# Second expert stage in three token groups instead of two, and the last expert block's result made by halves of its columns

## The chip, the cores and the metric

The kernel runs on one core of one Trainium2 chip. The core has a matrix engine (TensorE, PE in the profile, with its weight loads as PEld), VectorE (DVE), ScalarE (ACT), GpSimd (POOL) and SyncE (SP), which issues most of the transfers. Each engine works through its own list of instructions in order and waits for others by semaphores. The metric is the device time in microseconds (us) of one execution. A difference of about 1% is what a measurement of this kernel can tell from none.

## The reference

Three stages follow one another on 1536 tokens (2 x 768) of width 512:

```python
x = _attn_ref(q, k, v, n_sink, window)      # 8 heads of 64, a window of 128 and 4 sink keys
x = _moe_ref(x, w_skip, w_gate, w1, w2)     # first expert stage: 8 experts, 512 -> 1024 -> 512
h = x @ w_in                                # second expert stage: (1536, 512) @ (512, 2048)
g = np.where(h > 0.0, h, np.exp(np.minimum(h, 0.0)) - 1.0)
out = (g @ w_out).astype(np.float32)        # (1536, 2048) @ (2048, 512)
```

In the first expert stage a token with a positive skip score goes through the one expert that it scores highest on, and the gated result is added to it; the others stay as they are. `w_in` and `w_out` arrive as 64-bit floats, since the draw multiplies them by a 64-bit scalar.

## The kernel before

**First expert stage.** There are nine blocks of 128 tokens: one for each expert, and a ninth (number 8) for the tokens of one expert that did not fit. A block gathers its rows from the table `xtab` in DRAM, transposes them, makes the hidden layer in two halves (`layer1`, L902), applies the ReLU, makes the result in two halves of the hidden width (`layer2`, L918, the operations `b2`; all 512 columns in one PSUM bank), multiplies by the gate, and scatters the rows back to `xtab`. These matmuls are in float32, which TensorE runs as two records each.

**Second expert stage.** Each operand is split into a high and a low part in the type fp32r, and three products stand for one float32 product (`PASSES`). The 2048 hidden columns are 16 chunks of 128. The tokens are worked in groups (`GT`, 768 before, so two groups of six tiles of 128). For a group and a chunk, `l1` (L1083) makes the chunk's hidden values for the group's tokens, in two halves of 384 tokens (12 matmuls each, into one of two PSUM banks); five `elu` operations on ACT and DVE (L1095 or L1097, L1099, L1102, L1104, L290) turn them into the two parts of `gt`; `l2` (L1119, three matmuls of 512 columns for each token tile) adds the chunk's part to the six sums, which fill six banks for the whole group. `l2` of a chunk comes one chunk behind `l1`.

**Between the stages.** The first group's tokens do not wait for block 8's scatter. They are read from `xtab` before it (`lx0`, L986, two transfers of 384 rows), transposed into PSUM (`x0t`, L1016), and block 8's contribution is added there by matmuls with a one-hot matrix (`x0a`, L1021), which needs block 8's gated result as `delta` in two parts (L1000 on ACT, then L1002 on DVE). The sums are then split into `xT` (L1030 on ACT, L1032 on DVE). A later group's rows are loaded (L1040), transposed (L460 from L1042) and split (L1049, L1051) when the group before it is through `l1`.

**Weights of the second stage.** `w_in` and `w_out` are converted from 64-bit words on the chip, chunk by chunk: two loads (L736, L738), and for each of the two 128 x 512 halves one ACT operation (L960), five DVE operations (L962, L963, L964, L966, L290) and a cast (L968, ACT or DVE). The first ten chunks are converted beside the expert blocks, the rest beside the first group of the second stage.

**What sets the order.** Every operation is given to a planner (`Plan`) with its costs per engine, what it follows, a priority and the buffers that it takes. The planner goes through time and writes out one fixed order per engine; the chip keeps that order. `kinds` lists the buffers: `X`, `ACC` and `L1` are sets of PSUM banks, `g` and `r` rings in SBUF.

Of the kernel before, what the change touches and what calls it, by code (L numbers as in the profile page):

```python
# [8 lines left out]
F32 = mybir.dt.float32  # L9
F32R = mybir.dt.float32r  # L10
# [165 lines left out]
def fused_kernel(  # L176
# [28 lines left out]
    GT = 768  # L205
# [83 lines left out]
    def sub(o, a, b, e):  # L289
# [589 lines left out]
    def block(e):  # L879
# [16 lines left out]
        for n in range(2):  # L896
# [18 lines left out]
            def layer2(eng, n=n):  # L915
                for f in range(4 * n, 4 * n + 4):
                    w = w_tile(("w", e, KD + f // 2)).rearrange("p (c n) -> p c n", c=2)
                    nc.tensor.matmul(bk(("y", e)), sl(post["hT"], ("hT", e))[:, f, :], w[:, f % 2, :], start=(f == 0), stop=(f == KF - 1))  # L918
            add(("b2", e, n), {"e": 3.45}, layer2, [("relu", e, n)] + [("w", e, KD + 2 * n + i) for i in range(2)] + ([("b2", e, 0)] if n else []), p0 + 2 + n,
                need=[] if n else [("Y", ("y", e), 3 if last else 1)], use=[("hT", e)] + [("w", e, KD + 2 * n + i) for i in range(2)])  # L920
# [3 lines left out]
        add(("out", e), {"d": 0.69}, result, [("b2", e, 1)] + ([("dl", 0), ("dl", 1)] if last else []), p0 + 4, use=[("y", e), ("xg", e)])  # L924
# [50 lines left out]
    NS = NI // 2  # L975
    GH = GT // 2
    ohr = {}
    xTs = {}
    L8 = NB - 1

    def x0_tile():
        return post["exb"][:, 0:3072].rearrange("p (n j d) -> p n j d", n=2, j=NS)

    def load_x0(e, n):
        r0 = 1 + n * GH
        nc.sync.dma_start(out=x0_tile()[:, n], in_=xtab[r0:r0 + GH, 0:DM].rearrange("(j p) d -> p j d", p=P))  # L986

    def tokens_hot(e, n):
        if not n:
            post["oh"] = post["bp"].tile([P, 2 * GH], F32R, tag="c", name="oh")  # L990
        ohr[n] = post["oh"][:, n * GH:(n + 1) * GH]
        for j in range(NS):
            i = n * NS + j
            nc.vector.tensor_scalar(out=ohr[n][:, j * P:(j + 1) * P], in0=iota, scalar1=tok6[:, i:i + 1], scalar2=None, op0=ALU.is_equal)

    def delta(e, part):
        y, gt = bk(("y", L8)), gates(L8)
        if part == 0:
            post["dl"] = post["bp"].tile([P, 2, DM], F32R, tag="hs", name="delta")
            nc.scalar.activation(out=post["dl"][:, 0], in_=y, func=ACTF.Copy, scale=gt)  # L1000
        else:
            nc.vector.scalar_tensor_tensor(out=post["dl"][:, 1], in0=y, scalar=gt, in1=post["dl"][:, 0].bitcast(F32), op0=ALU.mult, op1=ALU.subtract)  # L1002
# [34 lines left out]
    for i in range(NI):
        def load_x(e, i=i):
            r0 = 1 + GT + i * P
            nc.sync.dma_start(out=post["row"][i][:, 0:DM], in_=xtab[r0:r0 + P, 0:DM])  # L1040
        add(("lx", i), {"s": 0.45}, load_x, [("scat", L8)] + [("cv", NCH - 1, w, 6) for w in range(2)] + ([("lx", i - 1)] if i else []), 310.0, size=262144)
        add(("xt", i), {"e": 0.44}, lambda e, i=i: four(post["row"][i], bk(("xt", i), 4), ident), [("lx", i)] + [("l1", 0, NCH - 1, i // NS)], 315.9 + 0.01 * i, need=[("L1", ("xt", i), 2)])  # L1042

        def x_ev(e, part, i=i):
            n, j = divmod(i, NS)
            m = bk(("xt", i), 4)
            o = xTs[n][:, :, :, j * P:(j + 1) * P]
# [464 lines left out]
```

## Time and profile before

| | us |
|---|---|
| median of three runs | 545.1 (543.37, 545.1, 547.71) |
| the profiled execution, its time | 546.95 |
| its span, first to last instruction | 545.2 |
| TensorE busy | 524.4 (96%) |
| VectorE busy | 317.8 (58%) |
| ScalarE busy | 190.1 (35%) |

Times in the rows are from the start of the span. The granted TensorE clock is 1.00 of full speed (2.4 GHz) throughout the stretches that are shown. In rows of a timeline, the second number is the length of the stretch from the first instruction's start to the last one's end; a bracket gives the idle time before it and what ended it. A matmul's own duration is longer than the step from one matmul to the next, because they are pipelined; steps are read as differences of starts.

### The profile page before, as it was taken

Reading aid. Unit: us, or ns where it says so; the run is one execution under the profiler, and the core shown is the slowest. Engines: PE = TensorE matmul, PEld = TensorE weight load, DVE = VectorE, ACT = ScalarE, POOL = GpSimd, SP = SyncE. Lnnn points to the kernel's source line nnn. Section 1 sums busy time; section 2 is a strip of 40 time slices with the busy share of each in tenths; the row PEclk is TensorE's granted clock in tenths of the full one; section 3 lists DMA queues with packets and bytes.
Section 4 is the critical chain, followed back from the end, with each engine's and each line's share of the span. In section 5 each row is a group of like instructions: output and inputs, shape, how many; then the busy total and the mean of one; then the engine's idle time right before and its main releaser. Section 6 shows DMA issues by size and latency. Waiting matters only on the chain.

```text
span 545.2 us, 8684 instructions
## 1 busy us (share of the span) xinstructions
PE 524.4 (96%) x3271; PEld 439.7 (81%) x3271; DVE 317.8 (58%) x887; ACT 190.1 (35%) x467; POOL 30.4 (6%) x46
## 2 busy tenths in 40 slices
PE   8999989988999999999899999999999999999994
PEld 4778767878777777777799899899989989999893
DVE  6777676875211468978999843433565344353442
ACT  3877566840000023433666521211232121121120
POOL 2000000011111011000001000000000000000000
PEclk9999998997999999999999999999999999999998
DMA  9999999319999868756545100000030000000003
GB/s 171 261 272 338 271 282 289 97 32 364 396 393 398 295 201 264 267 169 237 172 152 155 62 20 1 0 1 1 0 117 0 1 1 1 0 1 0 1 2 121
DMA packets 73141, 79.14 MB, mean 145 GB/s; under 512 B 43073, under 2 KB 51521, under 8 KB 73090
## 3 DMA queue, kind: packets, MB, share of 16 engines
q1 hardware_dynamic: 69810, 73.29, 43.3%
q0 software_dynamic: 1520, 4.99, 2.7%
q8 instruction: 28, 0.46, 0.4%
q10 hardware_dynamic: 1760, 0.22, 0.3%
q14 instruction: 23, 0.19, 0.1%
HBM read 69.82 MB, written 8.66 MB: 144 GB/s over the span
## 4 chain that ended last, share of the span: by engine, by line
PE 87%; DMA 9%; DVE 1%; ACT 1%; issue 1%; SPq 0%; ACTq 0%; DVEq 0%
PE bank L1083 24%; PE bank L1119 24%; PE bank L902 11%; PE bank L918 10%; DMA pl<-in_k_dram 4%; PE bank L572 4%; PE bank L531 4%; PE bank L460 3%; PE bank L603 2%; DMA raw<-in_moe_w_in_dram 2%; PE bank L559 1%; PE bank L577 1%; DMA pl<-in_q_dram 1%; PE bank L558 1%; DMA pl<-xtab,gid 1%; DMA xtab<-r,sidx 1%
## 5 line engine op out<-in xcount | busy, mean ns | idle before, releaser
L1083 PE MATMUL bank<-xT,m 128*128 128x384 f32 x768 | 139.3, 336 | 1.9 <-DVE xT L1051 1.0
L1083 PEld LDWEIGHTS bank<-xT,m 128*128 128x128 f32 x768 | 134.7, 188 | 4.8 <-ACT xT L1049 1.2
L1119 PE MATMUL bank<-m,gt 128*128 128x512 f32 x576 | 137.9, 392 | 0.0
L1119 PEld LDWEIGHTS bank<-m,gt 128*128 128x128 f32 x576 | 107.4, 188 | 21.0
L1099 ACT ACTIVATE re<-re 128x384 f32<-128x384 f32 x64 | 33.6, 525 | 143.7 <-DVE re L1097 142.7
L1097 DVE TENSOR_SCALAR re<-bank 128x384 f32<-128x384 f32 x28 | 15.6, 558 | 88.2 <-PE bank L1083 88.1
L902 PEld LDWEIGHTS bank<-blk,pl 128*128 128x128 f32 x480 | 57.1, 197 | 3.7 <-issue 2.6
L902 PE MATMUL bank<-blk,pl 128*128 128x128 f32 x480 | 58.0, 281 | 0.6 <-ACT blk L345 0.6
L918 PE MATMUL bank<-pl,blk 128*128 128x512 f32 x128 | 57.6, 592 | 0.0
L1102 DVE SCALAR_TENSOR_TENSOR re<-re,bank 128x384 f32<-128x384 f32 x64 | 35.4, 553 | 28.2 <-ACT re L1099 27.9
L545 ACT ACTIVATE pw<-sm,rm 128x272 f32<-128x272 f32 (+2 forms) x96 | 47.1, 495 | 7.0 <-DVE rm L537 7.0
L960 ACT ACTIVATE r<-raw 128x512 f32<-128x512 f32 x32 | 21.3, 678 | 62.4 <-DMA raw<-in_moe_w_in_dram 51.9
L918 PEld LDWEIGHTS bank<-pl,blk 128*128 128x128 f32 x128 | 23.1, 190 | 23.0 <-issue 23.0
L537 DVE CUSTOM_DVE_ANT_0 sm<-bank,mk 128x272 f32<-128x272 f32 (+2 forms) x96 | 35.2, 406 | 6.8 <-PE bank L531 4.8
L290 DVE TENSOR_TENSOR gt<-re,gt 128x384 fp32r<-128x384 f32 x61 | 34.0, 558 | 1.8
L1095 ACT ACTIVATE re<-bank 128x384 f32<-128x384 f32 x36 | 17.7, 491 | 32.4 <-PE bank L1083 32.4
L531 PE MATMUL bank<-kt,pl 64*128 64x272 f32 (+2 forms) x192 | 28.4, 418 | 0.0
L572 PE MATMUL bank<-PT,pl 128*64 128x128 f32 x352 | 25.2, 285 | 0.1
L345 ACT COPY PT<-bank 128x512 f32<-128x512 f32 (+1 forms) x40 | 20.6, 550 | 13.0 <-PE bank L559 10.7
L572 PEld LDWEIGHTS bank<-PT,pl 128*64 128x64 f32 x352 | 19.3, 139 | 5.9 <-issue 3.1
L966 DVE SCALAR_TENSOR_TENSOR r<-raw,r 128x512 int32<-128x512 int32 x32 | 22.6, 712 | 0.3
L290 DVE TENSOR_TENSOR m<-r,m 128x512 fp32r<-128x512 f32 x32 | 21.6, 689 | 1.6 <-ACT m L968 1.1
(186 smaller groups left out, 529.6 us busy)
## 6 DMA issues: line engine op xcount, KB each, us to landing
pl<-in_moe_w_dram SPq DMA_DIRECT2D x62, 512.0 KB
raw<-in_moe_w_in_dram SPq DMA_DIRECT2D x16, 512.0 KB
raw<-in_moe_w_out_dram SPq DMA_DIRECT2D x16, 512.0 KB
pl<-in_k_dram SPq DMA_DIRECT2D x12, 256.0 KB
pl<-in_q_dram SPq DMA_DIRECT2D x12, 256.0 KB
pl<-in_v_dram SPq DMA_DIRECT2D x12, 256.0 KB
xtab<-pl SPq DMA_DIRECT2D x12, 256.0 KB
out_dram<-raw SPq DMA_DIRECT2D x5, 512.0 KB
```

The costliest lines, as they stand in the source:

```text
L290: CE[e].tensor_tensor(out=o, in0=a, in1=b, op=ALU.subtract)
L531: nc.tensor.matmul(o, qT[r, p, :], rhs, start=True, stop=True)
L537: nc.vector.tensor_tensor_reduce(out=sl(sm_t, ("sm", t, h))[:, 0:n], in0=bk(("s", t, h))[:, 0:n], in1=m, scale=-scale, scalar=3.0e38, op0= ...
L545: nc.scalar.activation(out=sl(pw_t, ("pw", t))[:, h, 0:n], in_=sl(sm_t, ("sm", t, h))[:, 0:n], func=ACTF.Exp, bias=rm[:, t, h:h + 1], scal ...
L572: nc.tensor.matmul(o[i * D:(i + 1) * D, p, :], vt[:, h * D:(h + 1) * D], pT[:, (0 if y else c - 2) + i, :], start=(p == 0 and (y == 1 or n ...
L902: nc.tensor.matmul(o[:, i, :], w_tile(("w", e, kk))[:, f * P:(f + 1) * P], sl(post["xT"], ("xT", e))[:, kk, :], start=(i == 0 and kk == 0) ...
L918: nc.tensor.matmul(bk(("y", e)), sl(post["hT"], ("hT", e))[:, f, :], w[:, f % 2, :], start=(f == 0), stop=(f == KF - 1))
L966: add(nm(4), {"d": 0.69}, lambda e, ai=ai, r=r: nc.vector.scalar_tensor_tensor(out=ai(), in0=r()[:, :, 0], scalar=29, in1=ai(), op0=ALU.lo ...
L1083: nc.tensor.matmul(pt, w[:, a, kk, :], xTs[n][:, b, kk, :], start=(i == 0), stop=(i == 3 * KD - 1))
L1099: nc.scalar.activation(out=r, in_=r, func=ACTF.Exp, scale=-1.0)
L1102: nc.vector.scalar_tensor_tensor(out=r, in0=r, scalar=-1.0, in1=pt, op0=ALU.add, op1=ALU.max)
L1119: nc.tensor.matmul(bk(("acc", g, i)), gt[:, a, i % NS * P:(i % NS + 1) * P], w[:, b, :], start=(c == 0 and j == 0), stop=(c == NCH - 1 and ...
```

## The change

The group is 512 tokens, so there are three groups of four tiles. One `l1` operation then covers a whole chunk of a group: 12 matmuls of 512 columns. The sums of a group fill four banks (`ACC`, 0 to 3) and `l1` has four (`L1`, 4 to 7). `l2` gets the priority of two chunks behind `l1`; the ring `g` has three buffers of 512 tokens. `xT` is kept in six pieces, one for each 128 input columns (`XT`), so that a later group's pieces take turns with the earlier group's; `l1` is cut into two halves of the input columns for chunks 0 to 2 of the first group and chunk 0 of the others, so that its first half waits for two pieces only. A later group's transposes are placed within the last chunks of the group before, and its rows are loaded without waiting for the conversion of the weights.

In block 8 `layer2` is made in four pieces: both halves of the hidden width for result columns 0 to 255, then both for 256 to 511. `delta` and the one-hot matmuls follow by halves of the columns. The first group's rows come in one transfer of 512 rows.

```diff
-    GT = 768
+    GT = 512
...
-        S=B_(0, 1, 2, 3), T=B_(4, 5, 6, 7), O=B_(4, 5, 6, 7), HB=B_(0, 1, 2, 3), Y=B_(4, 5), T2=B_(6, 7), X=B_(*range(8)),
-        ACC=B_(0, 1, 2, 3, 4, 5), L1=B_(6, 7),
+        S=B_(0, 1, 2, 3), T=B_(4, 5, 6, 7), O=B_(4, 5, 6, 7), HB=B_(0, 1, 2, 3), Y=B_(4, 5), T2=B_(6, 7), X=B_(0, 1, 2, 3),
+        ACC=B_(0, 1, 2, 3), L1=B_(4, 5, 6, 7),
...
-        xg=ring(4, INF), xT=ring(2, INF), hT=ring(2, INF), a=ring(2, INF), r=ring(2), g=ring(5), row=ring(6, INF), o2=raws,
+        xg=ring(4, INF), xT=ring(2, INF), hT=ring(2, INF), a=ring(2, INF), r=ring(2), g=ring(3), XT=ring(6), row=ring(6, INF), o2=raws,
...
+            else:
+                add(("b2", e, 0) if n else ("b2x", e), {"e": 1.75}, lambda eng, n=n: layer2(eng, range(4 * n, 4 * n + 4), slice(0, DM // 2)), [("relu", e, n)] + ws + ([("b2x", e)] if n else []), p0 + 2 + n,
+                    need=[] if n else [("Y", ("y", e), 5)])
+                if n:
+                    for h in range(2):
+                        add(("b2", e, 1) if h else ("b2y", e), {"e": 1.75}, lambda eng, h=h: layer2(eng, range(4 * h, 4 * h + 4), slice(DM // 2, DM)), [("b2y", e) if h else ("b2", e, 0)], p0 + 4 + h,
+                            use=[("hT", e)] + [("w", e, KD + 2 * h + i) for i in range(2)])
...
-    for n in range(2):
-        add(("hot", n), {"d": 0.6}, lambda e, n=n: tokens_hot(e, n), ["tok6", "aend"], PB - 9)
-        add(("lx0", n), {"s": 0.45}, lambda e, n=n: load_x0(e, n), [("scat", L8 - 1), ("b2", 6, 1)], PB - 9, size=786432)
-    add(("dl", 0), {"a": 0.69}, lambda e: delta(e, 0), [("b2", L8, 1)], PB + 3.5, use=[("y", L8)])
-    add(("dl", 1), {"d": 0.74}, lambda e: delta(e, 1), [("dl", 0)], PB + 3.5, use=[("y", L8)])
+    add("hot", {"d": 0.9}, tokens_hot, ["tok6", "aend"], PB - 9)
+    add("lx0", {"s": 0.45}, load_x0, [("scat", L8 - 1), ("b2", 6, 1)], PB - 9, size=1048576)
+    for h in range(2):
+        add(("dl", 0, h), {"a": 0.37}, lambda e, h=h: delta(e, 0, h), [("b2", L8, h)], PB + 3.5, use=[("y", L8)])
+        add(("dl", 1, h), {"d": 0.41}, lambda e, h=h: delta(e, 1, h), [("dl", 0, h)], PB + 3.5, use=[("y", L8)])
...
+        def x0_add(e, a, kk=kk, key=key):
+            nc.tensor.matmul(bk(key), post["dl"][:, a, kk * P:(kk + 1) * P], post["oh"], start=False, stop=(a == 1))
+        add(("x0b", kk), {"e": 0.23}, lambda e, f=x0_add: f(e, 0), [("x0t", kk), "hot", ("dl", 0, kk // 2)], PB + 3.9 + 0.01 * kk)
+        add(("x0a", kk), {"e": 0.23}, lambda e, f=x0_add: f(e, 1), [("x0b", kk), ("dl", 1, kk // 2)], PB + 4 + 0.01 * kk)
+        split(0, kk, key, PB + 5 + 0.01 * kk, [("x0a", kk)] + ([("b2", L8, 1)] if kk > 1 else []))
...
+            add(("xt", g, kk), {"e": 0.44}, xt, [("lx", g, i) for i in range(NI)] + [("l1", g - 1, NCH - 1 - (kk < 2))], pr - 2.5 + kk * 0.6, need=[("L1", ("xt", g, kk), 2)])
+            split(g, kk, ("xt", g, kk), pr - 2.5 + kk * 0.6, [("xt", g, kk)])
...
+        if c < (1 if g else 3):
+            for h in range(2):
+                kks = (2 * h, 2 * h + 1)
+                add(name if h else ("l1k", g, c), {"e": 1.36}, lambda e, kks=kks: l1(e, kks),
...
-            add(("l2", g, c, i), {"e": 0.70}, l2, [("elu", g, c, i // NS, 4), ("cv", c, 1, 6)] + ([("l2", g, c - 1, i)] if c else []), p0 + 1.3 + 0.01 * i,
+            add(("l2", g, c, i), {"e": 0.68}, l2, [("elu", *key, 4), ("cv", c, 1, 6)] + ([("l2", g, c - 1, i)] if c else []), p0 + 2.3 + 0.01 * i,
```

The order that the planner writes is the same on every engine up to the end of block 8's hidden layer, but for two one-hot operations fewer on VectorE and one transfer in place of two. What it moves is shown at three places. In the changed kernel the lines are numbered otherwise: L1040 is the first group's transpose (L1016 before), L1044 the one-hot matmul (L1021), L1089 `l1` (L1083), L1127 `l2` (L1119), L1061 a later group's transpose (L460). `exb` holds the first group's rows, `blk` the hidden values of block 8, `m_` numbers a chunk's weights (the lowest number is chunk 0), `r_1488` to `r_1493` are row buffers.

TensorE at the end of block 8, before:

```order
L918 MATMUL bank_93<-pl_64,blk 128x512 x4
L1016 MATMUL bank_95<-ident,exb 128x128 x3
...
L918 MATMUL bank_93<-pl_65,blk 128x512 x4
L1016 MATMUL bank_94<-ident,exb 128x128 x3
...
L1021 MATMUL bank_95<-oh,delta 128x384 x2
...
L1083 MATMUL bank_95<-xT_2275,m_1874 128x384 x12
L1083 MATMUL bank_96<-xT_2275,m_1918 128x384 x12
L1083 MATMUL bank_95<-xT_2297,m_1874 128x384 x12
L1119 MATMUL bank_90<-m_1874,gt 128x512 x3
```

and in the changed kernel:

```order
L918 MATMUL bank_93<-pl_64,blk 128x256 x4
L918 MATMUL bank_93<-pl_65,blk 128x256 x4
L1040 MATMUL bank_90<-ident,exb 128x128 x4
...
L1044 MATMUL bank_91<-oh,delta 128x512
L918 MATMUL bank_93<-pl_64,blk 128x256 x4
L1044 MATMUL bank_90<-oh,delta 128x512
L1044 MATMUL bank_91<-oh,delta 128x512
L918 MATMUL bank_93<-pl_65,blk 128x256 x4
L1044 MATMUL bank_92<-oh,delta 128x512
L1044 MATMUL bank_89<-oh,delta 128x512
L1089 MATMUL bank_95<-xT_2269,m_1872 128x512 x6
L1044 MATMUL bank_92<-oh,delta 128x512
```

All 16 transposes now stand ahead of the last two quarters of block 8's result, the first columns' one-hot matmuls stand between these quarters, and nothing stands between the last quarter and the next columns' one-hot matmuls. From there `l1` of chunks 0 to 4 comes ahead of the first `l2`.

VectorE in the first group, while weights are still converted (L962 to L966 before are L972 to L976 now, L1102 is L1110), before and then in the changed kernel:

```order
L1102 SCALAR_TENSOR_TENSOR re<-re,bank_95 128x384
L966 SCALAR_TENSOR_TENSOR r_1493<-raw_83,r_1493 128x512
L962 TENSOR_SCALAR r_1492<-r_1492 128x512
L290 TENSOR_TENSOR gt<-re,gt 128x384
L290 TENSOR_TENSOR m_2337<-r_1493,m_2337 128x512
L963 TENSOR_SCALAR r_1492<-r_1492 128x512
L1102 SCALAR_TENSOR_TENSOR re<-re,bank_96 128x384
```

```order
L1110 SCALAR_TENSOR_TENSOR re<-re,bank_96 128x512
L290 TENSOR_TENSOR m_2384<-r_1492,m_2384 128x512
L974 SCALAR_TENSOR_TENSOR r_1493<-raw_85,r_1493 128x512
L290 TENSOR_TENSOR gt<-re,gt 128x512
L976 SCALAR_TENSOR_TENSOR r_1493<-raw_85,r_1493 128x512
L972 TENSOR_SCALAR r_1492<-r_1492 128x512
L1110 SCALAR_TENSOR_TENSOR re<-re,bank_94 128x512
L290 TENSOR_TENSOR m_2384<-r_1493,m_2384 128x512
L973 TENSOR_SCALAR r_1492<-r_1492 128x512
```

From one L1110 to the next there are now one `gt` and some five operations of a conversion (four in these rows, six in the next stretch), which is one half of a chunk's weights for each chunk of the group.

TensorE at the change of group, before and then in the changed kernel (`m_2665` and `m_2630` are the last chunk's weights):

```order
L1119 MATMUL bank_94<-m_2665,gt 128x512 x3
L460 MATMUL bank_96<-ident,r_1491 128x128 x4
L1119 MATMUL bank_92<-m_2665,gt 128x512 x3
L1119 MATMUL bank_89<-m_2665,gt 128x512 x3
L460 MATMUL bank_95<-ident,r_1492 128x128 x4
L1119 MATMUL bank_93<-m_2665,gt 128x512 x3
L460 MATMUL bank_96<-ident,r_1493 128x128 x4
L1083 MATMUL bank_95<-xT_2275,m_1874 128x384 x12
```

```order
L1061 MATMUL bank_95<-ident,r_1491 128x128
L1127 MATMUL bank_91<-m_2444,gt 128x512 x3
L1127 MATMUL bank_92<-m_2444,gt 128x512 x3
L1127 MATMUL bank_89<-m_2444,gt 128x512 x3
L1089 MATMUL bank_96<-xT_2269,m_2630 128x512 x9
...
L1061 MATMUL bank_93<-ident,r_1491 128x128
L1127 MATMUL bank_91<-m_2511,gt 128x512 x3
L1127 MATMUL bank_92<-m_2511,gt 128x512 x3
L1127 MATMUL bank_89<-m_2511,gt 128x512 x3
L1089 MATMUL bank_95<-xT_2301,m_1872 128x512 x6
```

Where the next group's `l1` came straight behind the last transpose, nine `l2` matmuls and more now stand between each pair of transposes and the `l1` that needs them.

## Rows read from the trace of the kernel before

**Rows 1.** The page: busy time of each engine, and the chain that ended last, by engine

```profile
PE 524.4 (96%) x3271; PEld 439.7 (81%) x3271; DVE 317.8 (58%) x887; ACT 190.1 (35%) x467; POOL 30.4 (6%) x46
PE 87%; DMA 9%; DVE 1%; ACT 1%; issue 1%; SPq 0%; ACTq 0%; DVEq 0%
```

**Rows 2.** Busy time by stretch: PE, PEld, DVE, ACT, POOL, clock, DMA share, GB/s

```profile
280.23:313.40 33.17, 33.17 (x170) 30.20 (x169) 29.73 (x57) 20.65 (x39) 3.61 (x3) 1.00 0.38 120
313.40:396.53 83.13, 83.13 (x423) 75.65 (x422) 35.69 (x71) 15.42 (x30) 0.00 (x0) 1.00 0.02 4
404.36:537.50 133.14, 133.10 (x672) 120.89 (x672) 59.15 (x117) 25.24 (x49) 0.00 (x0) 1.00 0.02 8
```

**Rows 3.** Chain that ended last, chunks 2 and 15 of the first group: start, us

```profile
280.23 4.18 PE bank L1083 x24
284.42 4.12 PE bank L1119 x18
...
388.20 4.18 PE bank L1083 x24
```

**Rows 4.** Who waited for whom, TensorE from 253 to 540: total, times, longest

```profile
PE bank L1083 <- DVE xT L1051: 1.0, 1, 1.0
PE bank L1083 <- DVE re L1102: 0.9, 1, 0.9
PE bank L1021 <- DVE delta L1002: 0.6, 1, 0.6
```

**Rows 5.** Timeline of block 8's end: start, us, engine, line, [idle before, releaser]

```profile
246.05 7.31 PE L902 MATMUL bank<-blk,pl 128*128 128x128 f32 x64
253.20 3.60 PE L918 MATMUL bank<-pl,blk 128*128 128x512 f32 x8
256.21 0.14 PEld L1016 LDWEIGHTS bank<-ident,exb 128*128 128x128 f32 x1 [0.24 <-DMA exb<-xtab]
256.63 1.47 PE L1016 MATMUL bank<-ident,exb 128*128 128x128 f32 x12
257.94 3.60 PE L918 MATMUL bank<-pl,blk 128*128 128x512 f32 x8
261.38 1.15 PE L1016 MATMUL bank<-ident,exb 128*128 128x128 f32 x9
261.64 0.67 ACT L1000 ACTIVATE delta<-bank,r 128x512 fp32r<-128x512 f32 x1
262.36 0.44 PE L1021 MATMUL bank<-oh,delta 128*128 128x384 f32 x1
263.37 2.53 PE L1021 MATMUL bank<-oh,delta 128*128 128x384 f32 x13 [0.57 <-DVE delta L1002]
266.42 4.35 PE L1083 MATMUL bank<-xT,m 128*128 128x384 f32 x24
271.62 2.37 PE L1083 MATMUL bank<-xT,m 128*128 128x384 f32 x12 [0.86 <-DVE re L1102]
```

**Rows 6.** Timeline of TensorE at the change of group

```profile
402.73 0.60 PE L460 MATMUL bank<-ident,r 128*128 128x128 f32 x4
404.36 1.81 PE L1083 MATMUL bank<-xT,m 128*128 128x384 f32 x9 [1.04 <-DVE xT L1051]
```

**Rows 7.** Groups by line, 253 to 282 us: busy, mean ns of one | idle before

```profile
L290 DVE TENSOR_TENSOR m<-r,m 128x512 fp32r<-128x512 f32 x8 | 5.4, 687 | 0.2
L962 DVE TENSOR_SCALAR r<-r 128x512 f32<-128x512 f32 x7 | 3.0, 423 | 1.0 <-ACT r L960 1.0
```

**Rows 8.** Groups by line, 380 to 546 us: ACT from PSUM, at two widths

```profile
L1132 ACT COPY raw<-bank 128x512 f32<-128x512 f32 x5 | 2.9, 586 | 5.5 <-PE bank L1119 5.1
L1129 ACT COPY raw<-bank 128x256 f32<-128x256 f32 x1 | 0.4, 372 | 1.5 <-PE bank L1119 1.5
```

**Rows 9.** Chain that ended last: the load issued behind L986's two

```profile
252.15 8.82 DMA raw<-in_moe_w_in_dram
```

**Rows 10.** Busy time as in rows 2, from L986's first issue to 256.21

```profile
251.14:256.21 5.07, 5.07 (x28) 3.40 (x28) 3.90 (x7) 2.52 (x4) 0.00 (x0) 1.00 0.67 222
```

More of the change, by code (lines that the diff above doesn't have):

```diff
@@ L913, in block, with layer2 @@
             add(("relu", e, n), {"a": 0.6, "d": 0.69}, relu, [("b1", e, n)] + ([("relu", e, 0)] if n else []), p0 + n, need=[] if n else [("hT", ("hT", e), 2)], use=[("h", e, n)])
[L915 to L920, printed above, removed]
+            def layer2(eng, fs, c):
+                for f in fs:
+                    w = w_tile(("w", e, KD + f // 2)).rearrange("p (c n) -> p c n", c=2)[:, f % 2, :]
+                    nc.tensor.matmul(bk(("y", e))[:, c], sl(post["hT"], ("hT", e))[:, f, :], w[:, c], start=(f == 0), stop=(f == KF - 1))
@@ new lines, in block @@
+            ws = [("w", e, KD + 2 * n + i) for i in range(2)]
+            if not last:
+                add(("b2", e, n), {"e": 3.45}, lambda eng, n=n: layer2(eng, range(4 * n, 4 * n + 4), slice(0, DM)), [("relu", e, n)] + ws + ([("b2", e, 0)] if n else []), p0 + 2 + n,
+                    need=[] if n else [("Y", ("y", e), 1)], use=[("hT", e)] + ws)
+            else:
[5 more added lines that the diff above has]
+                            use=[("hT", e)] + [("w", e, KD + 2 * h + i) for i in range(2)])
@@ L974, in fused_kernel @@
     NI = GT // P
[L975 to L978, printed above, removed]
     L8 = NB - 1
-    def x0_tile():
[L982 to L994, printed above, removed]
@@ L996, in delta, with piece, load_x0 @@
-    def delta(e, part):
-        y, gt = bk(("y", L8)), gates(L8)
+    xt_tiles = {}
+    def piece(g, kk):
+        i, j = divmod(pl.slot["XT", g, kk][1], 3)
+        if i not in xt_tiles:
+            t = post["bp"].tile([P, 3072], F32R, tag=("a", "xh")[i], name=f"xT{i}")
+            xt_tiles[i] = t.rearrange("p (j a n) -> p j a n", j=3, a=2)
+        return xt_tiles[i][:, j]
+    def x0_tile():
+        return post["exb"][:, 0:NI * DM].rearrange("p (j d) -> p j d", j=NI)
+    def load_x0(e):
+        nc.sync.dma_start(out=x0_tile(), in_=xtab[1:1 + GT, 0:DM].rearrange("(j p) d -> p j d", p=P))
@@ L998, in delta, with tokens_hot @@
+    def tokens_hot(e):
+        post["oh"] = post["bp"].tile([P, GT], F32R, tag="c", name="oh")
+        for i in range(NI):
+            nc.vector.tensor_scalar(out=post["oh"][:, i * P:(i + 1) * P], in0=iota, scalar1=tok6[:, i:i + 1], scalar2=None, op0=ALU.is_equal)
+    def delta(e, part, h):
+        c = slice(h * DM // 2, (h + 1) * DM // 2)
+        y, gt = bk(("y", L8))[:, c], gates(L8)
         if part == 0:
-            post["dl"] = post["bp"].tile([P, 2, DM], F32R, tag="hs", name="delta")
@@ L1037, in fused_kernel @@
[L1037 to L1047, printed above, removed]
+    add("hot", {"d": 0.9}, tokens_hot, ["tok6", "aend"], PB - 9)
@@ new lines, in layers, with l1 @@
+        key = (g, c)
+        name = ("l1", g, c)
+        def l1(e, kks):
+            w = ring2[c][:, 0].rearrange("p a (k f) -> p a k f", k=KD)
+            for kk in kks:
+                x = piece(g, kk)
+                for i, (a, b) in enumerate(PASSES):
+                    nc.tensor.matmul(bk(name), w[:, a, kk, :], x[:, b], start=(kk == 0 and i == 0), stop=(kk == KD - 1 and i == 2))
+        if c < (1 if g else 3):
+            for h in range(2):
+                kks = (2 * h, 2 * h + 1)
+                add(name if h else ("l1k", g, c), {"e": 1.36}, lambda e, kks=kks: l1(e, kks),
+                    [("xe", g, kk, part) for kk in kks for part in range(2)] + ([("l1k", g, c)] if h else [("cv", c, 0, 6)]), p0 + 0.01 * h,
+                    need=[] if h else [("L1", name, 2)], use=[("XT", g, kk) for kk in kks])
+        else:
+            add(name, {"e": 2.72}, lambda e: l1(e, range(KD)), [("l1", g, c - 1)] if g else [("cv", c, 0, 6)] + [("xe", g, kk, part) for kk in range(KD) for part in range(2)], p0, need=[("L1", name, 2)], use=[("XT", g, kk) for kk in range(KD)])
@@ new lines, in layers @@
+        L = lambda part: ("elu", *key, part)
+        first = [("dl", 1, 1)] + [(x, kk) for x in ("x0t", "x0b", "x0a") for kk in range(KD)] if s == 0 else []
+        add(L(0), {"a": 0.58, "d": 0.68}, lambda e: elu(e, 0), [name] + first, p0 + 0.2, need=[("r", ("r", *key), 2)], use=[name])
+        add(L(1), {"a": 0.64}, lambda e: elu(e, 1), [L(0)], p0 + 0.21)
+        add(L(2), {"d": 0.69}, lambda e: elu(e, 2), [L(1)], p0 + 0.22, use=[name])
+        add(L(3), {"d": 0.37, "a": 0.63}, lambda e: elu(e, 3), [L(2)], p0 + 0.23, need=[("g", ("g", *key), NI)], use=[("r", *key)], port=True)
@@ L1114, in layers @@
+        add(L(4), {"d": 0.62, "p": 1.4}, lambda e: elu(e, 4), [L(3)], p0 + 0.24, use=[("r", *key)], port=True, pen={"p": 0.5})
         for i in range(NI):
```

122 lines of the change are left out of this document (49 added, 73 removed).

## Prediction

> **What bounds the kernel now.** I read the page first: TensorE is busy 96% of the span and 87% of the chain that ended last is its work [rows 1], so only two things can move the time: what TensorE does, and where it waits. By stretch, the second expert stage is TensorE without a gap: 33.17 of 33.17 us, 83.13 of 83.13 and 133.10 of 133.14, at full clock [rows 2]. The chain shows its steps [rows 3]: 18 `l2` matmuls of 512 columns take 4.12 us, 0.2289 each; from the first `l1` shown to the last are 13 chunks in 107.97 us, 8.305 each, so 24 `l1` matmuls of 384 columns take 4.185, 0.1744 each. The list of waits leaves three for TensorE behind 253 us [rows 4]: block 8's `delta`, the third `l1`, which finds both its banks unread, and the last piece of `xT` at the change of group. Up to block 8's end (253.20) the order does not change, so the sum begins there.
>
> **What TensorE does.** *`l1`:* 768 matmuls x 0.1744 = 133.9 us become 48 chunks x 12 = 576. At 512 columns I take `l2`'s step: 576 x 0.2289 = 131.8, so **-2.1**. The least gain is a step that grows with the columns alone, 0.1744 x 512/384 = 0.2325 and 133.9, a gain of 0. *One-hot matmuls:* 16 x 0.1744 = 2.8 become 8 x 0.2289 = 1.8, **-1.0**. *`l2`* has 576 matmuls as before. *Transposes:* 24 + 24 become 16 + 2 x 16, the same 48; 12 take 1.31 us, 0.109 each [rows 5], **0**. *Block 8's result:* 16 float32 records of 512 columns (8 in 3.43 us, 0.429 each) become 32 of 256. The records of 128 columns step by 0.112 (64 from 246.05 to 253.20) [rows 5]; between them 256 columns give 0.218, 7.0 for 6.9 us, **+0.1** (0 if the halves cost exactly half).
>
> The first price has a rule against it. The two widths in the rows leave a part of 0.011 us per matmul that does not grow with the columns: (0.2289 - 0.1744)/128 is 0.426 ns a column, times 384 is 0.1635. The Trainium skill, "TensorE: Matmul & The Clock Gate", section "Back-to-back issue gap", gives a smaller fixed part, N/2.4 + 2.5 ns at full clock, with which `l1` would gain 192 x 2.5 ns = 0.5 us and the sum would be -3.3. The steps in the trace are longer than its 215.8 ns at 512 columns and 162.5 at 384, so I go by the rows.
>
> **Waits that go.** At `delta` the last matmul before the gap starts at 262.36 and has 0.17 of step; the next is at 263.37: 0.84 lost. At the third `l1`, 24 matmuls from 266.42 end at 270.61, the next is at 271.62: 1.01 [rows 5]. At the change of group four transposes from 402.73 take 0.44, the next `l1` is at 404.36: 1.19 [rows 6]. Together **-3.0**. The second goes because `l1` has four banks and chunk 0 is read out while chunks 1 to 4 are made. The third goes because behind each pair of transposes there are now 9 `l2`, and behind the second pair six `l1` and three `l2` more, ahead of the `l1` that needs that pair: 9 x 0.2289 = 2.1 us and, for the later pair, 4.1, against three operations of 0.69 in turn. What is late next there is the sums' banks: four reads of up to 0.69 on two engines, 1.4 us, beside 12 `l1` of 2.7 us that stand between.
>
> **Waits that come.** *Second half of `delta`.* Nothing stands between block 8's last quarter and the one-hot matmuls that need it. Before, from that place (261.38) to the first one-hot matmul were 0.98 us, with an ACT operation of 0.67 in them [rows 5]. At 256 columns an ACT read of PSUM is 586 - 372 = 214 ns shorter [rows 8]: 0.77. The VectorE half is hidden behind six `l1` (1.4 us). Bounds: 0, if the engines' overlap hid all of it, and 1.8, if it were the whole old wait without the transposes that filled 0.98 of it. I take **+0.8**. *One transfer of rows for two.* All 16 transposes now wait for 1049 KB, at 256.64. The first 786 KB had landed by 256.21, when the 0.24 us gap was the usual one [rows 5]; from the first issue to then 5.07 us x 222 GB/s = 1126 KB were moved [rows 10], so the larger transfer's bytes are through in time, but a completion trails. A load issued at 252.15 behind 1573 KB landed at 260.97, 8.82 us later [rows 9]; by the same lag (some 2 us behind its bytes) the rows would come at 258.0. Bounds 0 and 1.4; nearer the first transfer, which trailed by under 1 us: **+0.3**.
>
> **What is hidden.** The `elu` work of the first group lies beside the conversion of chunks 10 to 15 on VectorE, which is busy 29.7 of 33.2 us there [rows 2]. The order ties one half conversion to one chunk. An operation of 512 columns is 0.69, the fast ones 0.42 [rows 7]: three of 0.69 and two of 0.42 for the half, two of 0.69 for `elu`, 4.3 us, against 24 x 0.2289 = 5.5 on TensorE. `l2` at two chunks behind and `l1` of chunks 0 to 4 ahead of it give the first `elu` 8 us. SP's loads of later rows are queued between the weight loads and due 30 us or more later. Behind the conversion VectorE has four operations a chunk, 2.5 us at most. If this cover fails, see the slow rival.
>
> **Sum:** -2.1 - 1.0 + 0.1 - 3.0 + 0.8 + 0.3 = **-4.9 us**. The profiled execution took 546.95 for a span of 545.2; by it 542.0. It lies 1.85 above the median of the runs, 545.1, from which I forecast: **540.2**. With the bounds of the two new waits alone it is 538.7 (-6.4, with 0.35 of small gaps gone too) to 542.3.
>
> **Rivals.**
> *Width pays nothing* (chance 0.12). `l1`'s step grows with its columns, since the two widths of the rows belong to two lines with different operands. The 2.1 us stay: 542.3. For it: no row has `l1` at 512 columns. Against: both lines pair one weight load of 188 ns busy with each matmul, and show it only as overlapped. The skill's formula named above lies between, at 541.8.
> *A wait in the first layers* (0.10). VectorE is in order, and behind a late weight load an `elu` operation stands still. Worked through, `gt` of chunk 2 is ready some 2 us before its `l2`; a load that lands 3 to 5 us late eats that and costs 1 to 3 us once: 541.2 to 543.2, likeliest 542. For it: loads here take up to 8.82 us [rows 9]. Against: 500 KB less stand in front of them.
> *VectorE becomes the bound* (0.06), the case that ends slower. If a chunk of the first group had to wait for a whole conversion, VectorE would need 2 x 2.9 + 1.4 = 7.2 us for TensorE's 5.5; over chunks 10 to 15 that is 6 x 1.7 = 10 us: 550.3. It decides as soon as a chunk carries more than about 0.7 of a conversion; the order shows 0.5.
> *The halves do not overlap* (0.07). Both lie in one bank, so block 8's third quarter must wait until both `delta` reads of the first are through. The first columns are done at 256.7; ACT and VectorE need 0.46 and some 0.5, so 257.9, and TensorE comes there at 256.7 + 1.75 + 0.46 = 258.9. One conversion operation in front costs nothing, three cost 1 us: 541.2. The Trainium skill has this rule in "PSUM — Partial Sum Buffer", section "PSUM bank collisions raise a hardware error"; no run here shows a collision.
>
> **Numbers.** The forecast as summed has 0.65, the rivals 0.12, 0.10, 0.06 and 0.07. One per cent, about what a measurement of this kernel can tell from no change, is 5.45 us, or 539.65. The forecast lies 0.55 above that, its bounds reach 1 below and the three runs differ by 0.8%, so over half of its 0.65 falls within 1%: faster 0.38, same 0.56, slower 0.06. For 8 in 10 the range is 538.2 to 543.3: the forecast's own bounds and most of the three rivals beside them, with half a microsecond for the runs' spread.
>
> **What would show it.** Right: `l1` at 512 columns steps by 0.229; TensorE from 253.20 to the last `l2` takes some 279.4 us for 284.3; the only wait of TensorE over 0.5 us behind 253 is for `delta` on ACT, near 262.8; none at either change of group. Wrong: a step above 0.231; a wait of the transposes for `exb`, of `l2` for `gt` in chunks 0 to 9, or of block 8's third quarter for VectorE.

## The result, and the profile after

| | before | changed |
|---|---|---|
| median, first comparison (4 runs each), us | 544.66 | 538.39 |
| ratio and its 95% interval | | 0.9872 [0.9824, 0.9920] |
| median, second comparison (11 and 6 runs), us | 544.41 | 538.15 |
| ratio and its 95% interval | | 0.9893 [0.9867, 0.9920] |
| the profiled execution: time, span, us | 546.95, 545.2 | 538.53, 536.7 |

The changed kernel is 6.3 us faster (544.66 - 538.39, and 544.41 - 538.15), 1.1 to 1.3%. The forecast was 4.9 us, 540.2, with more than half of its chance on a difference of less than 1%. The waits and the one-hot matmuls came out close to their terms. The matmuls of the second stage gave 4.8 us where 2.1 were forecast.

The page of the changed kernel: busy time of TensorE and VectorE, which answer to [rows 1].

```profile
PE 512.6 (96%) x3087; PEld 411.5 (77%) x3087; DVE 317.5 (59%) x848; ACT 175.6 (33%) x421; POOL 32.2 (6%) x47
```

Busy time by stretch, columns as in [rows 2]: block 8's end, the rest of the first group, and two stretches of the later groups.

```profile
251.47:264.39 12.92, 12.36 (x64) 10.26 (x63) 11.90 (x23) 5.23 (x10) 0.66 (x1) 1.00 0.67 233
264.39:340.13 75.74, 75.74 (x340) 62.76 (x338) 56.49 (x103) 34.38 (x58) 0.84 (x2) 1.00 0.23 74
...
360.00:435.00 75.00, 75.00 (x341) 62.29 (x340) 35.86 (x58) 11.27 (x18) 1.29 (x1) 1.00 0.01 4
437.00:524.00 87.00, 87.00 (x386) 72.03 (x385) 41.19 (x66) 11.29 (x18) 0.00 (x0) 1.00 0.03 13
```

TensorE stands still only in the first of them, for 12.92 - 12.36 = 0.56 us. The list of waits of TensorE from 253 to 540 names that one and no other; of the three in [rows 4] none is left:

```profile
PE bank L1044 <- ACT delta L1013: 0.6, 1, 0.6
```

Block 8's end on TensorE, which answers to [rows 5]:

```profile
251.47 3.62 PE L918 MATMUL bank<-pl,blk 128*128 128x256 f32 x16
255.08 1.97 PE L1040 MATMUL bank<-ident,exb 128*128 128x128 f32 x16
256.80 0.71 PE L1044 MATMUL bank<-oh,delta 128*128 128x512 f32 x2
257.35 1.89 PE L918 MATMUL bank<-pl,blk 128*128 128x256 f32 x8
258.88 0.82 PE L1044 MATMUL bank<-oh,delta 128*128 128x512 f32 x2
259.54 1.89 PE L918 MATMUL bank<-pl,blk 128*128 128x256 f32 x8
261.99 0.73 PE L1044 MATMUL bank<-oh,delta 128*128 128x512 f32 x2 [0.56 <-ACT delta L1013]
262.56 1.54 PE L1089 MATMUL bank<-xT,m 128*128 128x512 f32 x6
263.94 0.62 PE L1044 MATMUL bank<-oh,delta 128*128 128x512 f32 x2
```

The 16 transposes start 3.61 us behind the first of 16 records. The engine does not fall idle there, but the weight load of the first transpose (PEld) waits for the rows in `exb`, and the step from the last of the records to this transpose is 0.367 where a record takes 0.216, so 0.15 us are lost:

```profile
255.08 1.73 PEld L1040 LDWEIGHTS bank<-ident,exb 128*128 128x128 f32 x16 [0.39 <-DMA exb<-xtab]
```

The one wait in the list is the forecast's: behind the last quarter, for `delta` on ACT. The change of group, [rows 6] before, and the steady part behind it:

```profile
342.85 0.85 PE L1127 MATMUL bank<-m,gt 128*128 128x512 f32 x3
343.54 1.04 PE L1061 MATMUL bank<-ident,r 128*128 128x128 f32 x8
344.33 2.30 PE L1127 MATMUL bank<-m,gt 128*128 128x512 f32 x9
346.47 1.52 PE L1089 MATMUL bank<-xT,m 128*128 128x512 f32 x6
347.83 0.84 PE L1127 MATMUL bank<-m,gt 128*128 128x512 f32 x3
348.51 1.52 PE L1089 MATMUL bank<-xT,m 128*128 128x512 f32 x6
349.87 2.20 PE L1127 MATMUL bank<-m,gt 128*128 128x512 f32 x9
351.91 2.88 PE L1089 MATMUL bank<-xT,m 128*128 128x512 f32 x12
354.63 1.75 PE L1127 MATMUL bank<-m,gt 128*128 128x512 f32 x7
```

No row has a bracket: where 1.19 us were lost, nothing is. The 12 `l1` from 351.91 to 354.63 take 2.72 us, a step of 0.2267. Of the later runs of 12 `l2`, which these rows do not show whole, each takes 2.72 too.

**Where the 7.8 us are.** The compared stretch runs from the start of block 8's first `b2` record to the start of the last `l2`: 283.88 us before, 276.08 in the changed kernel. Each matmul's step to the next, with the wait behind it, summed by line:

| line | before | changed | difference | forecast |
|---|---|---|---|---|
| `l1` (with the third `l1`'s wait) | 135.16 | 130.62 | -4.54 | -2.1 - 1.0 |
| `l2` | 132.01 | 130.75 | -1.26 | 0 |
| `b2` (with the waits behind it) | 6.87 | 7.60 | +0.73 | +0.1 + 0.8 + 0.3 |
| one-hot (with `delta`'s wait) | 3.81 | 2.23 | -1.58 | -1.0 - 0.84 |
| transposes (with the change of group) | 6.03 | 4.89 | -1.14 | -1.19 |
| sum | 283.88 | 276.08 | -7.8 | -4.9 |

In the `b2` line are 0.73 of wait for `delta` and 0.15 for the rows. The first one-hot matmul behind the third quarter starts 0.03 behind its last record, where a record's step is 0.216, and takes 0.19 longer to the next matmul; so 0.19 of that line are counted at the one-hot matmuls.

**What lies around it.** The two profiled executions differ by 8.5 us of span, because ahead of the first `b2` the changed one is 1.73 us shorter (251.47 for 253.20), and from the last `l2`'s start to the end 1.04 longer (9.09 for 8.05). Nothing shows the first to be the change's: the order of the work there is the same but for the few operations named with the change, and two profiles of the kernel before differ by more. TensorE ran at half of its 2.4 GHz in two stretches there before and in one afterwards, in the middle of first-stage work. Before, and below it the changed kernel:

```profile
82.00:86.00 4.00, 4.00 (x34) 2.62 (x31) 1.62 (x8) 2.42 (x11) 0.00 (x0) 0.67 1.02 381
122.00:126.00 4.00, 2.01 (x18) 1.90 (x17) 2.89 (x21) 0.06 (x1) 0.00 (x0) 0.95 0.93 263
126.00:132.00 6.00, 5.41 (x26) 5.13 (x26) 4.15 (x24) 0.58 (x1) 0.00 (x0) 0.50 1.05 383
```

```profile
82.00:86.00 4.00, 4.00 (x49) 3.23 (x46) 2.04 (x10) 3.94 (x14) 0.00 (x0) 1.00 0.96 365
120.00:124.00 4.00, 0.67 (x7) 0.45 (x5) 2.90 (x18) 0.22 (x1) 0.64 (x3) 0.96 0.72 215
124.00:128.00 4.00, 3.94 (x23) 3.72 (x21) 1.58 (x10) 0.03 (x1) 0.00 (x0) 0.61 0.98 307
```

The number behind POOL's is the granted clock. Ahead of the later stretch TensorE had been busy 2.01 of 4 us and 0.67 of 4. A second profile of the unaltered kernel before (below) has no such stretch and reaches its first `b2` at 250.22, for 253.20 here. So only the compared stretch and the end are set against each other from here on.

### The profile page after: what moved, and what is told of

Its sections match the earlier page's. It is cut to its first block, busy times and chain, and to the rows that moved or that the text cites. A ratio compares the mean times of both kernels' runs of the same rounds, so it can differ in the third digit from the quotient of the medians.

```text
span 536.7 us, 8226 instructions
## 1 busy us (share of the span) xinstructions
PE 512.6 (96%) x3087; PEld 411.5 (77%) x3087; DVE 317.5 (59%) x848; ACT 175.6 (33%) x421; POOL 32.2 (6%) x47
## 5 line engine op out<-in xcount | busy, mean ns | idle before, releaser
L1127 PE MATMUL bank<-m,gt 128*128 128x512 f32 x576 | 139.1, 390 | 0.0
L1089 PE MATMUL bank<-xT,m 128*128 128x512 f32 x576 | 138.3, 389 | 0.0
L1089 PEld LDWEIGHTS bank<-xT,m 128*128 128x128 f32 x576 | 108.1, 188 | 22.5
L1127 PEld LDWEIGHTS bank<-m,gt 128*128 128x128 f32 x576 | 107.8, 188 | 22.2
L1107 ACT ACTIVATE re<-re 128x512 f32<-128x512 f32 x48 | 30.3, 632 | 174.6 <-DVE re L1105 174.4
L1105 DVE TENSOR_SCALAR re<-bank 128x512 f32<-128x512 f32 x38 | 26.3, 692 | 83.7 <-PE bank L1089 83.7
L918 PE MATMUL bank<-pl,blk 128*128 128x512 f32 (+1 forms) x144 | 57.8, 545 | 0.0
L902 PE MATMUL bank<-blk,pl 128*128 128x128 f32 x480 | 56.1, 275 | 0.7 <-ACT blk L345 0.7
L1110 DVE SCALAR_TENSOR_TENSOR re<-re,bank 128x512 f32<-128x512 f32 x48 | 32.9, 686 | 26.5 <-ACT re L1107 26.5
L918 PEld LDWEIGHTS bank<-pl,blk 128*128 128x128 f32 x144 | 26.2, 190 | 20.9 <-issue 20.1
L290 DVE TENSOR_TENSOR gt<-re,gt 128x512 fp32r<-128x512 f32 x44 | 30.4, 692 | 1.3
L460 PE MATMUL bank<-ident,pl 128*128 128x128 f32 x96 | 14.8, 279 | 7.8 <-DMA pl<-in_k_dram 5.6
L976 DVE SCALAR_TENSOR_TENSOR r<-raw,r 128x512 int32<-128x512 int32 x32 | 21.8, 687 | 0.3
```

The costliest lines, as they stand in the source:

```text
L290: CE[e].tensor_tensor(out=o, in0=a, in1=b, op=ALU.subtract)
L902: nc.tensor.matmul(o[:, i, :], w_tile(("w", e, kk))[:, f * P:(f + 1) * P], sl(post["xT"], ("xT", e))[:, kk, :], start=(i == 0 and kk == 0) ...
L918: nc.tensor.matmul(bk(("y", e))[:, c], sl(post["hT"], ("hT", e))[:, f, :], w[:, c], start=(f == 0), stop=(f == KF - 1))
L1089: nc.tensor.matmul(bk(name), w[:, a, kk, :], x[:, b], start=(kk == 0 and i == 0), stop=(kk == KD - 1 and i == 2))
L1105: nc.vector.tensor_scalar(out=r, in0=pt, scalar1=-1.0, scalar2=0.0, op0=ALU.mult, op1=ALU.max)
L1107: nc.scalar.activation(out=r, in_=r, func=ACTF.Exp, scale=-1.0)
```

## The experiments

For each the stretch from the first `b2` record to the last `l2` is given; in two profiles of the changed kernel it is 276.08 and 276.25, and 0.16 of this difference is a longer wait for the rows (0.31 for 0.15). The 276.5 of some expectations runs to the end of the last `l2`, 0.39 behind its start.

**1. Is it the change of width that costs?** In the kernel before:

```diff
-            add(("l2", g, c, i), ..., p0 + 1.3 + 0.01 * i,
+            add(("l2", g, c, i), ..., p0 + (1.05 if i < NS else 1.3) + 0.01 * i,
```

> The kernel before, with l2 in two pieces between the two l1 halves (12 l1, 9 l2, 12 l1, 9 l2), so that the width changes four times a chunk instead of twice. Theory W (what the forecast missed is a loss at each change between 384 and 512 columns: a chunk before takes 8.305 us where 24 settled steps of 0.1735 and 18 of 0.2267 would take 8.244): the loss doubles to 0.12 a chunk, so a chunk takes 8.36 to 8.37 us and the 32 chunks 1.9 us more. Theory O (l2's 0.2289 is its own price, by its operands, its six banks or the other engines' reads beside it): a chunk stays at 8.305. The long steps stand behind each change by W, anywhere by O.

The stretch took 286.02. A piece of its timeline, TensorE in the steady part:

```profile
291.06 2.27 PE L1083 MATMUL bank<-xT,m 128*128 128x384 f32 x12
293.16 2.24 PE L1119 MATMUL bank<-m,gt 128*128 128x512 f32 x9
295.25 2.27 PE L1083 MATMUL bank<-xT,m 128*128 128x384 f32 x12
297.35 2.24 PE L1119 MATMUL bank<-m,gt 128*128 128x512 f32 x9
299.43 2.27 PE L1083 MATMUL bank<-xT,m 128*128 128x384 f32 x12
```

A chunk, from 291.06 to 299.43, takes 8.37, as theory W has it. On average 12 `l1` behind a change take 2.106 and 9 `l2` 2.079, against 4.186 for 24 and 4.121 for 18 before. A change to 384 columns so costs 0.025 and one to 512 columns 0.041 beside the settled step (that of matmuls well behind a change, worked out below), whether the run behind it is long or short: 2.106 is half of 4.186 and 0.013 more. Theory O falls. There are 118 such changes for 60. `l1` and `l2` together rose by 1.5 and not 1.9, because the kernel before also loses some 0.4 where transposes cut `l2` into short runs, and here they stand together. Another 0.5 is the wait at the change of group, 1.4 for 1.0. The ratio to the kernel before is 1.0052 [1.0027, 1.0078].

**2. What is the fixed part of a matmul?** In the changed kernel:

```diff
-            for kk in kks:
+            for n in [slice(0, 256), slice(256, 512)] if len(kks) == KD else [slice(0, 512)]:
+                for kk in kks:
...
-                    nc.tensor.matmul(bk(name), w[:, a, kk, :], x[:, b], ...
+                        nc.tensor.matmul(bk(name)[:, n], w[:, a, kk, :], x[:, b, n], ...
```

> The changed kernel, with l1 in two runs of 12 matmuls of 256 columns for 43 of the 48 chunks (the whole result is made). Theory F (each matmul has a fixed part of 13 to 14 ns beside 0.4167 ns a column, and each change of width costs 0.03 us): 256 columns step by 0.120, l1 of a chunk takes 2.89 instead of 2.72, with two changes a chunk goes from 5.44 to 5.67 us, and the 43 chunks take 9 to 11 us more: 548 to 549. Rival C (the step grows with the columns alone, the first rival of the prediction): 0.1133 a step, only the changes cost, +2.6 us: 541. Rival L (the weight load, 188 ns busy, bounds a short matmul): 0.188 a step, +1.8 us a chunk, 77 us in all.

The stretch took 284.23, 8.1 more, of which 0.3 are a longer wait for the rows. The time was 547.57 (1.0024 [0.9996, 1.0052] of the kernel before, so by time alone the two cannot be told apart). TensorE in the steady part:

```profile
303.87 3.04 PE L1090 MATMUL bank<-xT,m 128*128 128x256 f32 x24
306.74 2.91 PE L1128 MATMUL bank<-m,gt 128*128 128x512 f32 x12
309.49 3.04 PE L1090 MATMUL bank<-xT,m 128*128 128x256 f32 x24
```

24 `l1` take 2.87 (forecast by F 2.89), the chunk 5.62 (5.67). Their settled step is 0.1200. Settled steps of 0.1200, 0.1734 and 0.2267 at 256, 384 and 512 columns are 0.4167 ns a column and 13.3 ns in each. Rivals C and L fall. F's total was a little high, since only the way back to 512 columns costs (2.75 for 2.72); the first step at 256 columns is even shorter (0.113).

**3. What do block 8's halves give?** The changed kernel with `layer2`, `delta` and the one-hot matmuls of block 8 as before:

```diff
-                add(("b2", e, 0) if n else ("b2x", e), ..., slice(0, DM // 2)), ...
...
+                add(("b2", e, n), ..., layer2(eng, range(4 * n, 4 * n + 4), slice(0, DM)), ...
```

> The changed kernel with block 8's result, delta and their one-hot matmuls for all 512 columns at once, as before. If the halves pay as the forecast had it: behind the last b2 a wait of about 0.8 us beyond its step for delta on ACT, one of 0.1 to 0.3 for delta on VectorE, and one of 0.5 to 1.0 for the first split before l1, in place of the one wait of 0.56; from the first b2 to the last l2 1.0 to 1.8 us more than the 276.5 of the changed kernel: 539.4 to 540.2. If the halves pay nothing (the same reads, only cut): within 0.3 us of it.

The stretch took 278.76. Who waited for whom, TensorE:

```profile
PE bank L1034 <- DMA exb<-xtab: 1.7, 1, 1.7
PE bank L1038 <- ACT delta L1008: 0.8, 1, 0.8
PE bank L1083 <- DVE xT L1025: 0.2, 1, 0.2
```

The largest is the wait for the rows: they came 7.2 us after their issue, and the step to the first transpose, 0.43 without a wait, took some 1.9 us more. That the width in block 8 has no part in this is likely, since the load is issued some 2 us ahead of the first `b2` in both kernels, but one profile does not show it. Without it the stretch would be about 276.9, so by this estimate the halves are worth 0.6 to 0.8, less than the 1.0 to 1.8 expected: `delta` on ACT cost what was forecast, the split before `l1` less, and VectorE's `delta` nothing. By time, 541.10 us or 0.9916 [0.9885, 0.9947] of the kernel before, the interval overlaps that of the changed kernel.

**4. Can the new wait be filled?**

```diff
-        add(("x0t", kk), ..., ["lx0", ("b1", L8, 1)], PB + 2.5 + 0.01 * kk, ...
+        add(("x0t", kk), ..., ["lx0", ("b1", L8, 1)] + ([("b2", L8, 1)] if kk > 1 else []), PB + 2.5 + 0.01 * kk, ...
```

> The changed kernel with the eight transposes of input columns 256 to 511 behind the last quarter of block 8's result instead of ahead of the third. They take 0.87 us, about as long as the wait for delta's second half together with the step before it (start 259.54 of the last eight records to 261.99). If that wait is latency that other work can cover: it goes, and from the first b2 to the last l2 0.5 to 0.7 us less than 276.5 (538.39 to about 537.8). If something else is late at the same place (the gated columns, the banks): the wait stays and the order costs up to 0.9 more.

The stretch took 275.22, 0.86 less, and no idle time of TensorE is left in it:

```profile
256.18 1.89 PE L918 MATMUL bank<-pl,blk 128*128 128x256 f32 x8
257.90 1.04 PE L1040 MATMUL bank<-ident,exb 128*128 128x128 f32 x8
258.69 0.71 PE L1044 MATMUL bank<-oh,delta 128*128 128x512 f32 x2
```

Eight transposes stand where the wait was. By time (538.55, 0.9864 [0.9832, 0.9896] of the kernel before) it can't be told from the changed kernel.

**5. The changed kernel again, and a version that goes further.** The second has the edit of experiment 4 and also loads the rows by halves of the columns:

> The changed kernel itself, unaltered, beside two kernels derived from it, for a narrower interval. By the accounting of the first comparison the part behind the first b2 is 7.8 us shorter than before, and nothing ahead of it changed: a ratio of 0.9857 or so (537.2 for 545). By the forecast's sum of 4.9 it would be 0.991. In the profile, from the first b2 to the last l2: 276.1, or up to 1.7 more if the 1 MB of rows lands late, as it did in the run with full width in block 8.

```diff
-        nc.sync.dma_start(out=x0_tile(), in_=xtab[1:1 + GT, 0:DM].rearrange("(j p) d -> p j d", p=P))
+        d = slice(h * DM // 2, (h + 1) * DM // 2)
+        nc.sync.dma_start(out=x0_tile()[:, :, d], in_=xtab[1:1 + GT, d].rearrange("(j p) d -> p j d", p=P))
```

> The kernel that fills the wait (eight transposes behind the last quarter), and its rows loaded in two transfers, columns 0 to 255 of all 512 rows first, since the first eight transposes need only these. If the wait for the rows seen in some profiles (0, 0.3 and 1.7 us, 5.6 to 7.2 us after the issue) is that the bytes of the whole transfer come late: the first half lands 1 us or more earlier, no wait for exb over 0.1, and from the first b2 to the last l2 275.0 to 275.3 us; by time 0 to 0.5 us less than without. If the lag is not in the bytes (a fixed latency, or the 1 KB pieces go at half the pace): the first transposes wait as they do now, 0 to 1.7.

The changed kernel's stretch was 276.25, the further one's 275.20 without idle time of TensorE; their ratios 0.9893 [0.9867, 0.9920] and 0.9853 [0.9827, 0.9879], 538.15 and 536.56 us. The ratio expected of the changed kernel from its stretch alone, 0.9857, lies outside its interval; with the end 1.0 us longer it is about 0.9875, inside. The forecast's 0.991 lies inside too, so it is the profile and not the time that tells the two sums apart.

The further version has the lowest median here, but against experiment 4 its stretch is the same. The first half of the rows landed 4.4 us after its issue, for 5.6 there, and the step to the first transpose is 0.216, without a loss. TensorE then reaches the third quarter of block 8's result 0.1 us sooner, and its weight load waits for VectorE's `delta` of the first half, which reads the same bank:

```profile
PEld bank L918 <- DVE delta L1016: 0.3, 1, 0.3
```

About 0.15 us are lost there, as much as was gained ahead of it. That a late load can cost more is shown by experiment 3.

**6. What covers the change of group, and what the distance of two chunks gives.** First the transposes of later groups, with their splits, all behind the last `l1`, then `l2` one chunk behind:

```diff
-            add(("xt", g, kk), ... [("l1", g - 1, NCH - 1 - (kk < 2))], pr - 2.5 + kk * 0.6, ...
+            add(("xt", g, kk), ... [("l1", g - 1, NCH - 1)], pr - 0.1 + kk * 0.01, ...
```

> The changed kernel with a later group's 16 transposes all behind the last l1 of the group before, as in the kernel before, and not within its last chunks; l2 stays two chunks behind. If l2 at two chunks behind is what covers the change of group: nine l2 (2.04 us) stand behind the last transpose and ahead of the l1 that needs it, no wait over 0.3, and the part from the first b2 to the last l2 stays within 0.4 of 276.1. If it is the earlier place that does it: a wait of 1.0 to 1.3 at each of the two changes, 278.1 to 278.7.

```diff
-            add(("l2", g, c, i), ... p0 + 2.3 + 0.01 * i,
+            add(("l2", g, c, i), ... p0 + 1.3 + 0.01 * i,
```

> The changed kernel with l2 one chunk behind l1 instead of two. Between the end of a chunk's l1 and its l2 lie then 12 l2 and 12 l1, 5.44 us; its five operations take 0.60, 0.63, 0.69, 0.61 and 0.69, 3.2 us, and some 0.3 between them. Theory: no wait in the second and third group, a few in the first, where conversions stand between (0 to 3 us together), and one of 0.8 at the end, where only 12 l2 stand between the last l1 and its l2: 276.9 to 280. Rival (the second chunk of distance is needless): 276.1 within 0.3. Rival (VectorE is the bound of the first group as soon as the cover is short, the slow rival of the prediction): 6 us or more in the first group.

The stretches were 276.15 and 276.66, the ratio with late transposes 0.9871 [0.9836, 0.9906]. With late transposes TensorE does not stand still at the change of group: nine `l2` behind them are enough, and the earlier place was not needed. At one chunk behind, TensorE waits for no `gt` in the first group either; only at the very end the weight load of the last `l2` stands before it:

```profile
PEld bank L1127 <- DVE gt L290: 0.4, 1, 0.4
PEld bank L1127 <- DVE gt L1112: 0.3, 1, 0.3
```

So the waits expected in the first group did not come, and VectorE is not the bound there. The 276.66 lies between the theory's 276.9 and the rival's 276.1, since only the wait at the end came, with about 0.5 for 0.8. The end behind the last `l2` was also longer, 9.86 for 9.09; here the ratio is 0.9910 [0.9878, 0.9941].

**7. The kernel before again.**

> The kernel before, unaltered, for a second profile of it. If what stands around the compared part differs only by chance: from the first b2 to the last l2 again 283.9 within 0.2, the same l1 and l2 runs (4.186 and 4.121 us), and the end behind the last matmul 8.0 to 9.4 us, as in the nine profiles so far (8.05 to 9.86). If the change itself lengthened the end by 1 us: again 8.0 to 8.1.

The stretch took 283.63 (`delta`'s wait was 0.3 for 0.6), with the same runs, and the end 7.87. So the end was 8.05 and 7.87 before, 9.09 and 8.95 in the changed kernel; but it was 8.95 in experiment 1 as well, which is the kernel before with another place for half of its `l2`. The loads of instructions from the last `l2` to the end, first before, then changed (queue, loads, MB, share of the DMA engines):

```profile
q14 instruction: 6, 0.05, 2.0%
```

```profile
q14 instruction: 7, 0.06, 1.7%
```

In the eight profiles of the changed kernel and its variants SP stands 0.98 to 1.66 us at one of its last 26 semaphore instructions, always the tenth from the end. In the two of the kernel before and the one of experiment 1 it does not, and they have six loads. The seventh load is not what SP waits for: in the changed kernel SP stands from 6.56 to 8.02 us behind the last `l2`'s start, and the load begins at 8.58. What SP waits for stays open, and so does whether the change itself made the end longer, since experiment 1 has as long an end without it.

## Why the prediction was right and where it was wrong

**Right, by its own steps.** The three waits went as forecast: -3.0 by the rows before, and none of the three is in the list after. The new wait was placed and sized: +0.8 forecast, 0.73 found (the step from the last record to the next one-hot matmul is 0.943, less its own 0.216). ACT's `delta` of 256 columns took 0.47, forecast 0.67 - 0.21 = 0.46. `b2` by quarters costs nothing: 0.216 a record. The load of 1 MB, forecast at 0.3, cost 0.15 and 0.31 in the two profiles of the changed kernel; in the other variants with one load it cost 0.1 to 0.5, and 1.9 in experiment 3, above the bound of 1.4. The slow rival did not come: TensorE has no gap beside the conversion, even with `l2` at one chunk behind. Nor did the wait in the first layers: no `l2` waits for `gt`. Nor did the rival on the halves: both `delta` operations of the first half are through at 256.28, and the third quarter starts at 257.35; it shows in experiment 5, with 0.15.

**Wrong: the price of a matmul, in "What TensorE does".** The step said that at 512 columns `l1` takes `l2`'s step, 0.2289, and that `l2` has 576 matmuls as before, which put `l2` at 0. Both numbers of that step, 0.1744 and 0.2289, were means over whole runs, and each run in the kernel before begins behind a change of width. Its own timeline could have shown it. Here are the first and the last nine `l2` of one run, and the last 15 `l1` of the run behind it, in the kernel before:

```profile
317.48 2.24 PE L1119 MATMUL bank<-m,gt 128*128 128x512 f32 x9
...
319.56 2.20 PE L1119 MATMUL bank<-m,gt 128*128 128x512 f32 x9
...
323.19 2.76 PE L1083 MATMUL bank<-xT,m 128*128 128x384 f32 x15
```

The first nine take 319.56 - 317.48 = 2.08, 0.231 each. In the other two rows the last matmul's own duration, 0.389 or 0.334, is taken off the length: (2.20 - 0.389)/8 = 0.2264, and for `l1` (2.76 - 0.334)/14 = 0.1733. Step by step, the first matmuls behind the change run 0.229, 0.233, 0.236, 0.224, 0.231, 0.236, 0.228, 0.233, 0.230, and then 0.227 to the end. In the changed kernel `l1` and `l2` are both 512 wide; there is no change of width between them, and every run of 12 takes 2.720. It is not the change of operands or of line that costs, since these alternate as before.

So the error has one cause and counts twice: 0.0022 too much for 576 `l1` and for 576 `l2`, 1.3 us each. With the settled step `l1` gains 768 x 0.1744 - 576 x 0.2267 = 3.4 in place of 2.1, and `l2` 576 x 0.0022 = 1.3 in place of 0; in the table above they gave 3.5 (4.54 less the wait of 1.01) and 1.3. Of the 4.8 about 2.0 are the 60 changes of width, and 2.6 the fixed part of 192 matmuls, 13.3 ns each. With the settled step and 0.15 for the rows the sum is about -7.6, for -7.8 found. The measured time of 538.4 lies inside the range of 538.2 to 543.3 all the same, and that is luck: the stretch gained 7.8, more than the 6.9 of the range's lower end, and the end, which the sum left alone, came out 1.0 longer in these profiles.

**The rival on the width** had it that the step grows with the columns alone. Experiment 2 rules that out. The Trainium skill, "TensorE: Matmul & The Clock Gate", section "Back-to-back issue gap", has N/2.4 + 2.5 ns for a matmul taken by itself, and about 131 ns at 512 columns for a stream of weight loads and matmuls. The settled steps of these matmuls, each with its weight load, are N/2.4 + 13.3, 226.7 at 512 columns; so the measurement decides against both, and the smaller gain by the formula did not come.

**The chances** followed from the sum. With -4.9 the forecast lay at the bound of 1% and got 0.56 for no change; with the settled step in the same sum, and all else as it stands, it would have lain at -7.5 (-4.9 - 1.3 - 1.3), on the faster side.

## What to carry to other kernels

Take a matmul's step from matmuls in the middle of a run, one by one, never as the mean over a run that begins behind another shape; the difference is itself a cost, one per change, that goes when neighbours get the same width. Where a kernel is bound by TensorE, an error of 1% in the step of its main matmul is as large as several waits, so it deserves more care than they do. A wait that has just come up behind the last piece of a result is filled by moving independent work there, such as transposes that were done ahead.

## What was not expected of the hardware

- A change of matmul width costs: to 384 columns behind 512 0.025 us, back 0.041, over the first six to nine matmuls, whatever the length of the run. Why, the profile does not show.
- The 1 MB of rows, issued about 2 us ahead of the first `b2`, landed 5.6 to 5.8 us after its issue in five profiles and 7.2 in one.
- The end behind the last matmul took 7.9 to 8.1 us in two profiles of one kernel and 9.0 in one that gives half of its `l2` another place (experiment 1). Why, no run here shows.
